# Joint P*V bursts, one pool of work banks, a split first load and a new instruction order in a fused attention and feed-forward kernel

## The chip, the cores and the metric

The kernel runs on one core of one Trainium2 chip. The metric is the device time of one execution in microseconds (us), and lower is better. The profile's span is about 2 us shorter than that time, because it runs from the first recorded instruction to the last.

The engines appear by the profile's names. PE is TensorE (PEld is its weight load), ACT is ScalarE, DVE is VectorE, POOL is GpSimd and SP is SyncE, which issues most of the transfers. PSUM is the memory, in banks, that PE writes its results to. The granted clock is the share of the full clock rate that PE was given.

## The reference, cut to what matters

The input x has 2048 tokens of 512 values. Attention has 32 heads of 16 and runs over four segments of 512 tokens, with a memory matrix carried from segment to segment. A gated feed-forward layer of width 1792 uses the same x, and a sigmoid gate per token mixes the two results.

```python
g = _sigmoid((x * gate_w).sum(-1, keepdims=True))
# a: for each segment s of 512 tokens and each of the 32 heads
logits = einsum('bhqd,bhkd->bhqk', qs, ks) * scale + mask     # causal inside the segment
p      = softmax(logits)
a_dot  = einsum('bhqk,bhkd->bhqd', p, vs)                     # "P*V" below
a_mem  = (phi(qs) @ M) / (phi(qs) @ z + 1e-6)                 # "numerator", "denominator"
o      = sigmoid(beta) * a_mem + (1 - sigmoid(beta)) * a_dot
M, z   = M + phi(ks)^T vs, z + sum(phi(ks))
a      = o @ wo
# b: the feed-forward layer
b      = (gelu(x @ w_gate) * (x @ w_up)) @ w_down
return g * a + (1 - g) * b
```

## The kernel before

**A planner orders everything.** The program is a graph of tasks. When the kernel is built, a list scheduler simulates the five engines with an estimated duration for each task, and picks the next task again and again: the one that can start first, then the one of the highest priority. What it picks becomes the fixed order of each engine's instructions, and semaphores are derived from that order. A table of small priority corrections (`BIAS`) is the outcome of a search for a short plan. A wrong duration in this model costs nothing by itself. It costs when the order it produces makes an engine stand in front of something that is not ready.

```python
while len(order) < n:
    for e in ENGINES:
        for t in ready[e]:
            st = max(cur[e], ready_at[t.id])
            if t.tiled == "pv":                       # a P*V burst: at once after a QK fill, else late
                if last_pe == "qk" and ready_at[t.id] <= cur[e]:
                    best = ((-1.0, 0.0, t.id), e, t)
                    continue
                st += t.patience
            if t.grp is not None and t.grp.bank is None:   # needs a free PSUM bank
                if not bank_free: continue
                st = max(st, min(bank_free.values()))
            k = (st, -t.prio - ..., t.id)
            ...
    if t.nbytes:
        dma_free = max(t.finish + 1.5, dma_free) + t.nbytes / DMA_RATE
```

**Attention.** A group of eight heads is handled as two units of four heads. Five "fills" of Q*K products (A0, B0, C, A1, B1) go to the four score banks. Each is followed by one exponential of 128x2048 on ACT, which writes a "P tile" to on-chip memory, and by a causal mask on POOL. C serves both units. P*V of a unit is 16 matmuls into one private PSUM bank `Pb`, followed by a DVE transpose.

```python
R_PT = 6; N_W = 3                                  # six P tiles, three work banks
Pb = psum_tensor("psP", [P, 512], F32)             # P*V's own bank
def pv(j, sa, sbk, sc):
    for kb in range(4):
        for q in range(4):
            matmul(Pb[32*q:32*q+17, 128*kb:512], Vaug[...], PT[slot][...],
                   tile_position=(0, 32*q))        # four tiles of 32 columns side by side
    task(transpose of Pb into Tb[t % 2] on DVE)
a0 = fill("A0", ...); b0 = fill("B0", ...); cc = fill("C", ...)
pv(0, a0, b0, cc)
a1 = fill("A1", ...); b1 = fill("B1", ...)
pv(1, a1, b1, cc)
norm()
```

Three tilings of the array alternate on PE: four row tiles for Q*K, four column tiles for P*V, and the whole array for everything else.

**Start.** PE runs ten warming matmuls (columns of zeros) while x arrives, transposes x, runs three more of them, and then makes the first K and Q products. Beta and the gate row are needed in odd layouts, and they are loaded by many tiny pieces on ACT's queue.

```python
wdma("wk", SP, wk[:], r4(A_wk), 524288)
wdma("wq", SP, wq[:], r4(A_wq), 524288)
wdma("wv", SP, wv[:], r4(A_wv), 524288)
wdma("beta", ACT, betab[:], A_beta.partition_broadcast(P), 8192)
for g in range(4):      # pieces of two values, 4 bytes
    bsrc = A_beta.rearrange("(t g j) -> g t j", g=4, j=2)[g]
    dma(f"betaT{g}", ACT, betaT[32*g:32*g+32, :]..., bsrc.partition_broadcast(32), 1024)
wdma("gatew", ACT, gatew[:], gate_w.rearrange("(kb p) -> p kb", p=P), 1024)   # one value, 2 bytes
```

The softmax here doesn't subtract the row's maximum and nothing guards it: scores larger than these inputs give would overflow.

## Time and profile before

| Quantity | Before | Seen in |
|---|---|---|
| median time | 293.34 us (293.33 to 293.64) | timed runs |
| traced span | 290.8 us | profile page |
| PE busy | 272.3 us, 94% | profile page |
| ACT busy, next after PE | 217.5 us, 75% | profile page |
| first exponential starts | 16.66 us | timeline |
| PE busy from 120 to 150 us | 24.88 of 30 us | windows |

These are lines of the profile page of the kernel before: busy microseconds of each engine; the busy tenths of PE and its granted clock in 40 slices of 7.3 us; and the shares, by engine, of the chain of work that ended last.

```profile
PE 272.3 (94%) x2150; PEld 114.2 (39%) x2189; DVE 191.3 (66%) x332; ACT 217.5 (75%) x172; POOL 103.0 (35%) x193
PE   6699999999999899996799999999999999999995
PEclk9899999999999999999799999999999999999999
PE 79%; DVE 9%; ACT 5%; DMA 3%; issue 2%; POOL 1%; SPq 0%; ACTq 0%
```

PE bounds the kernel: it is busy nearly always, and the chain that ended last is four fifths PE. There are two soft places, slices 1 and 2 (0 to 15 us) and slices 19 and 20 (131 to 145 us). In both the clock drops too.

The next lines are the largest waits of PE in the kernel before: what PE waited to do, for whom, the sum, the number of times and the longest.

```profile
PE psW L421 <- DVE otok L677: 3.4, 3, 2.1
PE psXALL L730 <- ACT pt L738: 2.6, 5, 1.5
PE psW L421 <- DMA wq<-in_A_wq_dram: 2.0, 1, 2.0
PE psW L516 <- DMA hT<-in_A_x_dram: 1.5, 1, 1.5
```

`otok` is the scaled numerator of the attention memory, and `hT` at the start serves as the landing place of x. The timeline of the kernel before gives start, length, engine and line, output and inputs, and in brackets the idle time before and who ended it.

```profile
7.20 0.73 PE L516 MATMUL psW<-ident,hT 128*128 128x128 bf16 x10 [1.47 <-DMA hT<-in_A_x_dram]
9.11 1.04 PE L421 MATMUL psW<-xT,wk 128*128 128x512 bf16 x4
12.19 1.89 PE L421 MATMUL psW<-xT,wq 128*128 128x512 bf16 x4 [2.04 <-DMA wq<-in_A_wq_dram]
...
137.16 0.39 PE L730 MATMUL psXALL<-qT,kpad_1 32*128 32x512 bf16 x4 [1.51 <-ACT pt L738]
...
139.61 2.34 PE L421 MATMUL psW<-xT,wu 128*128 128x512 bf16 x5 [2.05 <-DVE otok L677]
```

Four matmuls of the same form take 1.04 us at 9.11 and 1.89 us at 12.19. The difference is the clock, as the windows show. The windows give start and end in us, the length, busy time (and instructions) of PE, PEld, DVE, ACT and POOL, the granted clock, the DMA share and GB/s.

```profile
0.00:30.00 30.00, 24.72 (x156) 9.69 (x159) 15.05 (x33) 16.11 (x18) 11.52 (x33) 0.94 0.89 244
120.00:150.00 30.00, 24.88 (x232) 10.54 (x235) 25.11 (x42) 21.60 (x19) 9.81 (x13) 0.94 0.09 19
12.00:14.00 2.00, 1.81 (x5) 0.71 (x6) 0.80 (x4) 0.96 (x2) 0.00 (x0) 0.55 0.88 282
```

From the view of the transfers of the kernel before, ACT's queue q10 (packets, MB, share of the 16 engines' span) and two transfers (number, size, median us from issue to landing) matter in the argument. Only the tiny loads are on q10.

```profile
q10 hardware_dynamic: 1248, 0.01, 0.2%
...
hT<-in_A_x_dram SPq DMA_DIRECT2D x2, 256.0 KB, 5.0
...
wq<-in_A_wq_dram SPq DMA_DIRECT2D x1, 512.0 KB, 9.8
```

### The profile page before, as it was taken

The page shows a single profiled execution, that of the slowest core. Times are in us where ns is not written, and L with a number is a line of the kernel's source. Part 1 is how long each engine was busy: PE and PEld are TensorE (multiplying, and loading weights), DVE is VectorE, ACT ScalarE, POOL GpSimd, SP SyncE. Part 2 cuts the span into 40 slices and gives each one's busy share as a digit, 9 for nine tenths or more (in the row PEclk, how much of TensorE's full clock was granted, in tenths as well). Part 3 has the DMA queues.
Part 4 walks back from the last instruction along what each step waited for, and adds up shares of the span by engine and source line. Part 5 has one row for each costly group of instructions (what it writes and reads, how often), then busy time and mean ns, then how long its engine had stood idle before and what let it go on. Part 6 is the DMA issues. An engine that isn't in the chain of part 4 may idle for free.

```text
span 290.8 us, 5337 instructions
## 1 busy us (share of the span) xinstructions
PE 272.3 (94%) x2150; PEld 114.2 (39%) x2189; DVE 191.3 (66%) x332; ACT 217.5 (75%) x172; POOL 103.0 (35%) x193
## 2 busy tenths in 40 slices
PE   6699999999999899996799999999999999999995
PEld 2234343343455343432244343344344434533342
DVE  0378898885887947899451926299980767772432
ACT  2377898888998767986668878789787767777722
POOL 8015864344006353343200334366420243343320
PEclk9899999999999999999799999999999999999999
DMA  3999990000005541000200121000000000211002
GB/s 88 285 246 342 280 102 2 0 1 2 0 2 72 73 109 38 1 0 20 54 2 0 36 38 36 10 29 2 0 2 0 1 3 0 48 45 38 19 2 72
DMA packets 29737, 15.30 MB, mean 53 GB/s; under 512 B 21264, under 2 KB 29712, under 8 KB 29712
## 3 DMA queue, kind: packets, MB, share of 16 engines
q1 hardware_dynamic: 28464, 14.95, 22.5%
q8 instruction: 17, 0.28, 0.4%
q10 hardware_dynamic: 1248, 0.01, 0.2%
q14 instruction: 8, 0.07, 0.1%
HBM read 8.14 MB, written 2.10 MB: 35 GB/s over the span
## 4 chain that ended last, share of the span: by engine, by line
PE 79%; DVE 9%; ACT 5%; DMA 3%; issue 2%; POOL 1%; SPq 0%; ACTq 0%
PE psW L421 64%; PE psXALL L730 8%; PE psP L763 6%; ACT pt L738 5%; DMA wq<-in_A_wq_dram 3%; PE psXALL L421 1%; DVE tb L771 1%; DVE kpad_1 L617 1%; DVE hT L861 1%; DVE otok L677 1%; POOL pt L750 1%; DVE kT L597 1%; DVE ost L889 0%; SPq L452 0%; DVE pex L595 0%
## 5 line engine op out<-in xcount | busy, mean ns | idle before, releaser
L738 ACT ACTIVATE pt<-psXALL 128x2048 bf16<-128x2048 f32 x80 | 150.1, 1877 | 42.6 <-PE psXALL L730 27.9
L750 POOL TENSOR_SCALAR_AFFINE_SELECT pt<-pt 128x512 bf16<-128x512 bf16 (+1 forms) x112 | 83.2, 745 | 172.4 <-ACT pt L738 151.7
L421 PE MATMUL psW<-xT,wu 128*128 128x512 bf16 x216 | 52.1, 386 | 2.8 <-DVE otok L677 2.1
L861 DVE TENSOR_TENSOR hT<-psW,hT 128x512 bf16<-128x512 f32 x56 | 37.1, 686 | 26.3 <-PE psW L421 26.1
L421 PE MATMUL psW<-xT,wg 128*128 128x512 bf16 x217 | 50.7, 380 | 0.8 <-ACT hT L840 0.2
L421 PE MATMUL psW<-wd,hT 128*128 128x512 bf16 x203 | 50.5, 380 | 0.5 <-issue 0.2
L771 DVE STREAM_TRANSPOSE tb<-psP 128x512 f32<-128x512 f32 x32 | 22.9, 714 | 31.7 <-PE psP L763 31.4
L421 PEld LDWEIGHTS psW<-xT,wu 128*128 128x128 bf16 x224 | 20.5, 99 | 29.0 <-issue 3.3
L421 PEld LDWEIGHTS psW<-xT,wg 128*128 128x128 bf16 x224 | 20.5, 98 | 25.5 <-issue 1.7
L421 PEld LDWEIGHTS psW<-wd,hT 128*128 128x128 bf16 x210 | 18.8, 98 | 22.4 <-issue 3.3
L763 PE MATMUL psP<-pt,vaug 128*17 128x256 bf16 (+3 forms) x512 | 23.3, 301 | 0.6 <-POOL pt L750 0.6
L840 ACT ACTIVATE hT<-psW 128x512 bf16<-128x512 f32 x28 | 16.4, 597 | 6.7 <-PE psW L421 6.7
L421 PE MATMUL psW<-xT,wq 128*128 128x512 bf16 x59 | 16.3, 397 | 2.6 <-DMA wq<-in_A_wq_dram 2.0
L730 PE MATMUL psXALL<-qT,kpad_1 32*128 32x512 bf16 (+3 forms) x256 | 15.8, 301 | 2.6 <-ACT pt L738 2.6
L421 PE MATMUL psW<-xT,wk 128*128 128x512 bf16 x61 | 16.2, 396 | 0.3 <-DVE sc_1 L785 0.2
L421 PE MATMUL psW<-wv,xT 128*128 128x512 bf16 x61 | 15.7, 381 | 0.3 <-DVE vaug L438 0.2
L438 DVE CAST hT<-psW 128x512 bf16<-128x512 f32 x20 | 13.5, 683 | 3.8 <-PE psW L421 3.4
L730 PE MATMUL psXALL<-qT,kpad_0 32*128 32x512 bf16 (+3 forms) x256 | 15.8, 301 | 0.1
L763 PEld LDWEIGHTS psP<-pt,vaug 128*17 128x17 bf16 x512 | 10.0, 89 | 14.0 <-issue 5.9
L645 POOL COPY exsT<-exs 32x4 f32<-32x4 f32 x64 | 14.1, 220 | 3.7
L421 PE MATMUL psW<-wo,oT 128*128 128x512 bf16 x54 | 14.6, 380 | 0.6 <-issue 0.3
L829 ACT ACTIVATE hT<-hT 128x2048 bf16<-128x2048 bf16 (+2 forms) x6 | 12.7, 2185 | 0.0
(93 smaller groups left out, 242.5 us busy)
## 6 DMA issues: line engine op xcount, KB each, us to landing
out_dram<-ost SPq DMA_DIRECT2D x16, 128.0 KB, 1.7
wg<-in_B_w_gate_dram SPq DMA_DIRECT2D x2, 896.0 KB, 13.1
wu<-in_B_w_up_dram SPq DMA_DIRECT2D x2, 896.0 KB, 7.0
wd<-in_B_w_down_dram SPq DMA_DIRECT2D x1, 1792.0 KB, 13.0
hT<-in_A_x_dram SPq DMA_DIRECT2D x2, 256.0 KB, 5.0
wk<-in_A_wk_dram SPq DMA_DIRECT2D x1, 512.0 KB, 7.2
wq<-in_A_wq_dram SPq DMA_DIRECT2D x1, 512.0 KB, 9.8
wv<-in_A_wv_dram SPq DMA_DIRECT2D x1, 512.0 KB, 12.5
```

Of the source, the lines that this page charges most:

```text
L421: return Instr(lambda e: e.matmul(view(), lhsT, rhs, start=first, stop=last), reads=reads, writes=[fkey if fkey is not None else g.key], e ...
L438: alts[DVE] = [Instr(lambda e: e.tensor_copy(dst(), src()), reads=reads, writes=writes, est=dve_t(n))]
L597: Instr(lambda e: e.tensor_tensor(dst[:, t0:t1, :], dst[:, t0:t1, :], ex[:], ALU.add), dk + [("pex", i)], dk, dve_t(1024, 2))])
L645: cross = task(f"exsT{s}", POOL, [Instr(lambda e, g=g, c=c: e.tensor_copy(exsT[sl][32 * g:32 * g + 32, c:16:4], exs[32 * c:32 * c + 32, s4 ...
L730: instrs.append(Instr(lambda e, t=t, g=g, j=j, kb=kb, ncol=ncol, c0=c0: e.matmul(X[g][:, c0:c0 + ncol], kpad[j][sl][32 * g:32 * g + 32, t, ...
L738: prev_exp[0] = exp_task(s, f"exp{s}_{t}{name}", [Instr(lambda e: e.activation(PT[slot][:], XALL[:, :].rearrange("p (g c) -> p g c", g=4), ...
L750: minstrs.append(Instr(lambda e, view=view, pat=pat: e.affine_select(out=view, in_=view, compare_op=ALU.is_ge, fill=0.0, base=0, pattern=p ...
L763: instrs.append(Instr(lambda e, q=q, kb=kb, slot=slot, c0=c0, h=h: e.matmul(Pb[32 * q:32 * q + 17, 128 * kb:512], Vaug[sl][:, kb, h, :], P ...
L771: task(f"pvt{s}_{t}_{j}", DVE, [Instr(lambda e: e.transpose(Tb[i2][:, j, :], Pb[:, :]), [("P",)], [("Tb", i2, j)], dve_t(512))])
L829: t = task(f"gelu{s}_{f0}", ACT, [Instr(lambda e, hv=hv: e.activation(hv, hv, ACTF.Gelu_apprx_tanh), hk, hk, act_t(512 * n, False) + (0.0 ...
L840: lambda e, g=g, ft=ft, s=s: e.activation(hT[s % 2][:, ft, :], g.f32()[:, :], ACTF.Gelu_apprx_tanh),
L861: task(f"Um{s}_{ft}", DVE, [Instr(lambda e, g=g, ft=ft: e.tensor_tensor(hT[sl][:, ft, :], g.f32()[:, :], hT[sl][:, ft, :], ALU.mult), [g.k ...
```

## The change

The intent is to remove changes of tiling by running both units' P*V as one burst, to let every product use any of four work banks, to bring the first pieces of `wk` and `wq` early, to replace the tiny loads by contiguous ones that are spread on chip, and to give the planner truer durations and a new order.

```diff
-R_PT = 6
-N_W = 3
+R_PT = 7
+N_W = 4
-BIAS = { ... }
+BIAS = { ... }                       # wholly new: found anew
# planner: durations
-    cur = {e: 0.0 for e in ENGINES}
+    cur = {e: 0.8 for e in ENGINES}
-    dma_free = max(t.finish + 1.5, dma_free) + t.nbytes / DMA_RATE
+    dma_free = max(t.finish + 2.2, dma_free) + t.nbytes / DMA_RATE
-    Instr(lambda e: e.reciprocal(nf, nf), [("nd",)], [("nd",)], 0.3),
+    Instr(lambda e: e.reciprocal(nf, nf), [("nd",)], [("nd",)], 0.95),
# ... four more durations corrected
# planner: P*V may follow Q*K or P*V, takes a bank of the pool, and a ready pair keeps banks free
-    if last_pe == "qk" and ready_at[t.id] <= cur[e]:
+    if last_pe in ("qk", "pv") and ready_at[t.id] <= cur[e] and bank_free and \
+            min(bank_free.values()) <= cur[e]:
# P*V
-    Pb = psum_tensor("psP", [P, 512], F32)
+    gp = Grp(banks)                  # in pv(): any bank of the four
-    pv(0, a0, b0, cc)
     a1 = fill("A1", ...); b1 = fill("B1", ...)
-    pv(1, a1, b1, cc)
+    joint = [S.tasks[-1]]            # both wait for the last fill's mask
+    pv(0, a0, b0, cc, joint)
+    pv(1, a1, b1, cc, joint)
# start
-    wdma("wk", SP, wk[:], r4(A_wk), 524288)
-    wdma("wq", SP, wq[:], r4(A_wq), 524288)
+    for c0, c1 in ((0, 128), (128, 512)):
+        for key, w, src in (("wk", wk, A_wk), ("wq", wq, A_wq)):
+            wdma((key, c0 > 0), SP, w[:, :, c0:c1], r4(src)[:, :, c0:c1], ...)
-    wdma("beta", ACT, ...); 4 x dma("betaT", ACT, ...); wdma("gatew", ACT, ...)
+    wdma("gwrow", SP, gwrow[:], gate_w.rearrange("(kb p) -> kb p", p=P), 16384)   # transposed by PE
+    wdma("beta", SP, betab[:], A_beta.partition_broadcast(P), 65536)   # POOL copies make omgT
# x is transposed in the idle score banks; four of the warming matmuls go
-    x0t: g = Grp(banks) ...   -warmP, -warmE (3)
+    x0t: XB[:, kb*1024 + ...] with key ("X", kb)
```

## The prediction

> **What bounds the kernel.** TensorE. The page has PE busy 272.3 of 290.8 us and the chain of waits is 79% PE. ACT is next (217.5 us; 80 exponentials of 1.88 us = 150.1). So PE time counts: waits, slow clock, and mode switches inside "busy".
>
> Reading PE by stretches of the span (table of windows, and PE's own timeline):
> - 0 to 12.2 us: 7.2 busy. PE waits 1.47 us for x and 2.04 us (10.15 to 12.19) for `wq`, whose DMA lands 9.8 us after issue. After that hole the granted clock is 0.55 to 0.59 from 12 to 16 us: about 1.7 us more. The first exponential starts at 16.7 us.
> - 12 to 120 us: about 3.2 us of small waits.
> - 120 to 150 us: 24.9 of 30 busy, clock 0.94: holes of 1.51 and 2.05 us at 137 and 139.6 us, where the numerator products hold all three work banks and wait for DVE (`otok` copies behind a 0.95 us reciprocal that the old plan estimates at 0.3). About 5 us of wait, 1.2 us of slow clock.
> - 150 to 270 us: about 2 us. Tail after the last matmul: about 3 us.
>
> **What the change does.**
> 1. *Joint P*V.* A QK fill occupies PE 0.32 us before the next work, of which four concurrent tiles of 512 columns need 0.213; a P*V burst occupies 0.65 for 1280 columns (0.533). So each change of tiling costs about 0.11 us, in agreement with the Trainium skill, "TensorEngine Tiling (Array Packing)", Key Properties: changing the mode drains the engine. 32 bursts become 16 pairs: 16 x 0.11 = 1.8 us, all on PE, critical.
> 2. *Four shared banks.* Projections, gate, up and down products get a fourth bank while no P*V is open, but a pair takes two until its two 0.72 us transposes finish. Small net gain.
> 3. *Corrected durations and a new order.* I expect the 120 to 150 us hole to go mostly and new small ones to appear: 3 us net.
> 4. *Start.* The first 128 columns of `wk` and `wq` arrive first, so the first Q product can follow the first K product without the 2.04 us wait, and the clock should stay up: up to 3.7 us. Against it: 256-byte rows, more descriptors, three warming matmuls gone, `wv` later. Net 3 us. The tiny pieces for beta and gate leave the queues; exponentials start about 4 us earlier.
> 5. *Losses.* The last pair's two transposes run one after the other before the last normalisation: +0.7 us in the tail, partly covered by the last down products. New GpSimd copies and the single `Tb` are off the path (DVE 66% busy).
>
> Sum: 1.8 + 0.5 + 3 + 3 - 0.7 = 7.6 us off 293.3.
>
> **Prediction: 285.7 us, range 281.5 to 290. Faster by over 2%: 0.70; within 2%: 0.27; slower: 0.03.**
>
> **What would show it.** (1) P*V groups in pairs of about 1.2 us, 16 of them; (4) first `wq` matmul near 10 us, clock not below 0.9 from 10 to 16 us, first exponential near 12.5 us; (3) PE busy over 28.5 of 30 us in every 30 us window of the middle; (5) last matmul to end of span as before, or under 1 us more. PE idle over the span should fall from 18.5 to about 12 us.
>
> **What would make it wrong.** The clock drops anyway in the start because the warmers are gone or the rest of `wk`/`wq` (768-byte rows) lands late; the pair, which waits for both units' exponentials and masks and for two banks, makes PE or ACT stall elsewhere; the new order merely moves the mid holes.

## The result, and the profile after

The kernel after takes **278.41 us** (278.16 to 278.99, four runs), against 293.33 us in the same rounds (293.25 to 293.64). The ratio is 0.9492, with a 95% interval of 0.9476 to 0.9509. That is 14.9 us saved, where 7.6 us had been predicted; the measured time lies 3 us below the range.

These lines of the page of the kernel after answer to those of the page before.

```profile
PE 265.9 (96%) x2147; PEld 114.8 (41%) x2186; DVE 196.7 (71%) x336; ACT 213.1 (77%) x166; POOL 101.5 (37%) x197
PE   8999999999999999999999999999899999999995
PEclk9999999999999999999999999999999999999999
PE 81%; ACT 6%; DVE 4%; POOL 2%; issue 2%; DMA 2%; SPq 1%; DVEq 0%; ACTq 0%; POOLq 0%
```

Both soft places are gone and the clock is full wherever it was recorded. (The trace's clock records begin at 5.5 us, and at 5.4 us before; earlier the view shows 1.00 without one, while in both kernels the warming matmuls start 0.43 us apart, against 0.22 later on.) PE still bounds the kernel. PE idle fell from 18.5 to 10.8 us, and PE busy fell by 6.4 us: slow-clock matmuls and changes of tiling sit inside "busy". The two together are the 14.1 us of span.

These are the largest waits of PE in the kernel after; "issue" means that the profile shows nothing that PE waited for.

```profile
PE psW L430 <- issue: 2.7, 17, 0.2
PE psW L513 <- DVE pt L488: 1.3, 1, 1.3
PE psW L430 <- DVE hT L873: 1.1, 3, 0.6
PE psXALL L741 <- ACT pt L749: 0.5, 2, 0.3
PE psW L430 <- DMA wq<-in_A_wq_dram: 0.3, 1, 0.3
```

After the start almost nothing is left to wait for. The first line is mostly not real: these 17 gaps of 0.16 us are places where the record of one matmul is missing (of the program's 937 matmuls of 512 columns over the whole array, the trace has 898). The timeline of the kernel after shows the start, and then one joint pair with such a gap behind it.

```profile
5.07 1.27 PE L518 MATMUL psXALL<-ident,hT 128*128 128x128 bf16 x16
...
6.36 0.61 PE L430 MATMUL psW<-xT,wk 128*128 128x512 bf16 x2
...
6.80 0.59 PE L430 MATMUL psW<-xT,wq 128*128 128x512 bf16 x2
...
52.40 1.26 PE L774 MATMUL psW<-pt,vaug 128*17 128x512 bf16 x32
...
53.59 0.55 PEld L430 LDWEIGHTS psW<-xT,wg 128*128 128x128 bf16 x4 [0.16 <-issue]
53.83 0.81 PE L430 MATMUL psW<-xT,wg 128*128 128x512 bf16 x3 [0.16 <-issue]
```

x is transposed 2.1 us earlier than before, and the first Q product comes at 6.80 instead of 12.19 us. The pair of P*V occupies PE from 52.40 to about 53.6 us, 1.20 us. Behind it four weight loads stand against three matmuls: the fourth matmul ran and was not recorded.

The windows of the kernel after, for the same two long stretches as before:

```profile
0.00:30.00 30.00, 28.06 (x220) 12.20 (x225) 19.57 (x42) 21.59 (x22) 19.32 (x63) 1.00 0.98 288
120.00:150.00 30.00, 28.60 (x262) 13.53 (x263) 21.33 (x42) 22.77 (x24) 10.73 (x32) 1.00 0.09 19
```

The start has gained 3.3 us of PE busy time in 30 us and the stretch from 120 to 150 us 3.7. These are the same two transfers in the kernel after; that of `wq` is its first part.

```profile
hT<-in_A_x_dram SPq DMA_DIRECT2D x2, 256.0 KB, 3.0
...
wq<-in_A_wq_dram SPq DMA_DIRECT2D x1, 128.0 KB, 4.4
```

**An account of PE's loss.** From the length of each stretch I took off the time that its matmuls need merely to stream their columns (0.216 us for an ordinary matmul of 512 columns, a quarter of that where four tiles run side by side). Matmuls without a record were counted from the program's order. What is left is loss: waits, slow clock and changes of tiling.

| Stretch | lost before | lost after |
|---|---|---|
| 0 to 20 us | 9.8 us | 4.8 us |
| 20 to 120 us | 10.8 us | 8.2 us |
| 120 to 150 us | 9.45 us | 3.1 us |
| 150 us to the end | 14.5 us | 15.1 us |

Four warming matmuls fewer add 0.9 us, since before they counted as work. So 5 to 6 us came from the start, 6 from the stretch from 120 to 150 us, and about 2 from the rest.

### The profile page after: what moved, and what is told of

Its sections match the earlier page's. It is cut to its first block, busy times and chain, and to the rows that moved or that the text cites. A ratio compares the mean times of both kernels' runs of the same rounds, so it can differ in the third digit from the quotient of the medians.

```text
span 276.7 us, 5333 instructions
## 1 busy us (share of the span) xinstructions
PE 265.9 (96%) x2147; PEld 114.8 (41%) x2186; DVE 196.7 (71%) x336; ACT 213.1 (77%) x166; POOL 101.5 (37%) x197
## 4 chain that ended last, share of the span: by engine, by line
PE 81%; ACT 6%; DVE 4%; POOL 2%; issue 2%; DMA 2%; SPq 1%; DVEq 0%; ACTq 0%; POOLq 0%
PE psW L430 65%; PE psXALL L741 8%; PE psW L774 6%; ACT pt L749 5%; DMA wq<-in_A_wq_dram 2%; PE psXALL L430 1%; POOL exsT L656 1%; SPq L461 1%; POOL pt L761 1%; DVE hT L873 1%; ACT L852 1%; DVE ost L901 1%; DVE tb L782 0%; ACT hT L852 0%; DVE ndsc L678 0%
## 5 line engine op out<-in xcount | busy, mean ns | idle before, releaser
L761 POOL TENSOR_SCALAR_AFFINE_SELECT pt<-pt 128x512 bf16<-128x512 bf16 (+1 forms) x112 | 81.1, 727 | 156.0 <-ACT pt L749 134.0
L430 PE MATMUL psW<-xT,wu 128*128 128x512 bf16 x216 | 51.3, 380 | 1.4 <-DVE hT L873 0.6
L873 DVE TENSOR_TENSOR hT<-psW,hT 128x512 bf16<-128x512 f32 x56 | 37.3, 685 | 15.2 <-PE psW L430 13.6
L782 DVE STREAM_TRANSPOSE tb<-psW 128x512 f32<-128x512 f32 x32 | 21.1, 697 | 21.6 <-PE psW L774 21.4
L774 PE MATMUL psW<-pt,vaug 128*17 128x256 bf16 (+3 forms) x512 | 20.4, 300 | 0.2 <-ACT hT L852 0.2
L430 PE MATMUL psW<-xT,wq 128*128 128x512 bf16 x59 | 15.7, 380 | 0.8 <-DMA wq<-in_A_wq_dram 0.3
L430 PE MATMUL psW<-wo,oT 128*128 128x512 bf16 x57 | 15.1, 380 | 0.2
L656 POOL COPY exsT<-exs 32x4 f32<-32x4 f32 x64 | 13.8, 216 | 3.7
L774 PEld LDWEIGHTS psW<-pt,vaug 128*17 128x17 bf16 x512 | 10.7, 90 | 10.5 <-issue 3.5
L901 DVE TENSOR_SCALAR ost<-psW,omgt 128x512 bf16<-128x512 f32 x10 | 7.3, 748 | 9.8 <-PE psW L430 9.8
```

What stands on the lines that cost most here:

```text
L430: return Instr(lambda e: e.matmul(view(), lhsT, rhs, start=first, stop=last), reads=reads, writes=[fkey if fkey is not None else g.key], e ...
L656: cross = task(f"exsT{s}", POOL, [Instr(lambda e, g=g, c=c: e.tensor_copy(exsT[sl][32 * g:32 * g + 32, c:16:4], exs[32 * c:32 * c + 32, s4 ...
L761: minstrs.append(Instr(lambda e, view=view, pat=pat: e.affine_select(out=view, in_=view, compare_op=ALU.is_ge, fill=0.0, base=0, pattern=p ...
L774: instrs.append(Instr(lambda e, q=q, kb=kb, slot=slot, c0=c0, h=h: e.matmul(gp.f32()[32 * q:32 * q + 17, 128 * kb:512], Vaug[sl][:, kb, h, :],
L782: task(f"pvt{s}_{t}_{j}", DVE, [Instr(lambda e: e.transpose(Tb[:, j, :], gp.f32()[:, :]), [gp.key], [("Tb", j)], dve_t(512))], grp=gp)
L873: task(f"Um{s}_{ft}", DVE, [Instr(lambda e, g=g, ft=ft: e.tensor_tensor(hT[sl][:, ft, :], g.f32()[:, :], hT[sl][:, ft, :], ALU.mult), [g.k ...
```

## The experiments

All experiments except four keep an order. For these, the planner's choice was replaced by a list of (task, engine, bank), recorded from the kernel before or after. The list reproduces that kernel exactly, so that only the edit differs. There is one exception: in `b_tiny`, `b_start` and `b_both` the work on beta of ACT and DVE also moves behind the first copies of K and Q. In the kernel before ACT waits 2.86 us for the beta pieces, until 11.58 us, before it copies the first K product; PE's wait for `wq`, until 12.19 us, ends later.

```diff
-    for t in S.schedule():
+    for t in S.replay(ORDER):       # ORDER: the recorded choice of the kernel before, or after
```

In the other four ("order found anew") the search for `BIAS` was run again. "Saved" is (1 - ratio) times 293.34 us. Each ratio is against the kernel before in the same rounds. Four executions stand behind each row, three behind the row of `a_pair1`.

| Run | Base, order | Edit | Median us | Ratio [95%] | Saved us |
|---|---|---|---|---|---|
| after | | the whole change | 278.41 | 0.9492 [0.9476, 0.9509] | 14.9 |
| b_tiny | before, kept | small loads as in the change | 289.86 | 0.9887 [0.9869, 0.9905] | 3.3 |
| b_split | before, kept | `wk`, `wq` split | 295.38 | 1.0072 [1.0031, 1.0113] | -2.1 |
| b_start | before, kept | both | 290.49 | 0.9911 [0.9889, 0.9933] | 2.6 |
| b_pool | before, kept | P*V in one pool of four banks | 289.82 | 0.9883 [0.9865, 0.9901] | 3.4 |
| b_both | before, kept | start and pool | 285.79 | 0.9753 [0.9713, 0.9793] | 7.2 |
| b_retuned | before, anew | true durations | 291.21 | 0.9917 [0.9879, 0.9955] | 2.4 |
| b_start_retuned | before, anew | true durations and start | 281.00 | 0.9571 [0.9532, 0.9610] | 12.6 |
| b_retuned_oldstart | that order, kept | old start put back | 286.77 | 0.9774 [0.9735, 0.9813] | 6.6 |
| a_pair1 | after, kept | pairs apart by 1 piece | 281.64 | 0.9597 [0.9581, 0.9613] | 11.8 |
| a_pair2 | after, kept | pairs apart by 2 pieces | 282.13 | 0.9616 [0.9600, 0.9632] | 11.3 |
| a_unsplit | after, kept | `wk`, `wq` whole | 283.61 | 0.9665 [0.9627, 0.9703] | 9.8 |
| a_addtiny | after, kept | old small loads added on ACT | 283.56 | 0.9678 [0.9647, 0.9710] | 9.4 |
| a_tinylate | after, kept | the same on SP, behind `wv` | 283.35 | 0.9650 [0.9601, 0.9698] | 10.3 |
| a_addbetaT | after, kept | only the beta pieces added | 281.36 | 0.9581 [0.9543, 0.9619] | 12.3 |
| a_oldstart | after, kept | old start put back | 288.85 | 0.9836 [0.9791, 0.9881] | 4.8 |
| a_nojoin | after, anew | P*V not joint | 279.71 | 0.9531 [0.9500, 0.9563] | 13.8 |
| a_oldtimes | after, anew | old durations | 280.94 | 0.9579 [0.9548, 0.9611] | 12.3 |

The theories were these. J: a joint pair is worth its saved changes of tiling, some 0.1 us each as predicted. S: the start is worth more than predicted, and it is the tiny pieces (rival: the split of `wk` and `wq`) that make it so. O: the plan with true durations holds on the chip, where the old plan did not (rival: the pool of banks alone cures the hole at 120 to 150 us).

### The start, one half at a time, in the order of before

```diff
# b_tiny
-    wdma("beta", ACT, ...); 4 x dma("betaT", ACT, ...); wdma("gatew", ACT, ...)
+    wdma("gwrow", SP, ...); wdma("beta", SP, ...)      # behind wv; spread on chip as in the change
# b_split
-    wdma("wk", SP, wk[:], ...); wdma("wq", SP, wq[:], ...)
+    wk[:, :, 0:128], wq[:, :, 0:128], wk[:, :, 128:512], wq[:, :, 128:512]     # four loads
# b_start: both
```

> The kernel before with its order of work kept as a fixed list, and only the beta and gate loads changed as in the change (one row load each behind wv on the SP queue, spread on chip); no split of wk and wq. Theory T (the tiny loads on the second queue held up the x and weight loads): x is transposed from about 5 us instead of 5.5 to 8.6, the first wk matmul starts near 7 instead of 9.1 us, total 1.5 to 2.5 us less (near 291). Rival S (only the order of wk and wq matters): x and wk land as before, total within 0.5 us of 293.3.

> The kernel before, order kept, and only wk and wq loaded in two parts (first 128 columns of both first). Rival S: first wq matmul follows the first wk one with no wait, clock stays up, total about 3.5 us less (near 290). Theory T: x still ends near 8.5 us, so about 2 us less, the rest needs the tiny loads gone.

> The kernel before, order kept, with both start changes. The account of PE time lost in the first 20 us is 9.8 before and 4.8 after, plus 0.9 for four warming matmuls that stay here. If the start is worth what this account says and all of it reaches the end, total 4 to 5.5 us less (288 to 289). If work later absorbs it (a fixed order tuned for a late start), under 2.5 us less.

Without the tiny pieces x lands 2.9 us after issue instead of 5.0, and 3.3 us are saved. The transfers of `b_tiny`:

```profile
hT<-in_A_x_dram SPq DMA_DIRECT2D x2, 256.0 KB, 2.9
```

The split alone makes the kernel 2.1 us slower. With the tiny pieces still there, `wv` lands 9.4 us after its issue, PE then waits 2.0 us for it at 15.2 us, and the clock falls to 0.50 from 16 to 20 us. Both halves together save 2.6 us in this order, no more than the small loads alone. The mean granted clocks of the timed runs show where some of it goes. The time lost to the clock, (1 - clock) times the span, is about 3.5 us before, 1.7 in `b_tiny`, 5.3 to 7.1 in `b_split` and 3.5 to 3.8 in `b_start`. That is enough to account for all that the split lost, and for `b_start` not beating `b_tiny`. The soft stretch from 120 to 150 us is not healed: in `b_start` PE is as busy there as before, and the clock is 0.89 instead of 0.94.

```profile
120.00:150.00 30.00, 24.95 (x209) 9.89 (x211) 21.90 (x38) 20.14 (x19) 8.14 (x11) 0.89 0.09 19
```

### The pool of banks, in the order of before

```diff
-N_W = 3                          Pb: private
+N_W = 4                          gp = Grp(banks) in pv(), as in the change
# b_both: this and b_start's edit
```

> The kernel before, order kept, P*V takes its bank from one pool of four (no joint bursts, six P tiles). Theory P (the hole of 120 to 150 us in the kernel before is a shortage of banks): the waits for otok at 97 and 139 us shrink, total about 2 to 3 us less. Rival O (the hole comes from the order and the DVE chain, banks matter little once the order is fixed): within 1 us of before.

> The kernel before, its order kept, with both start changes and the pool of four banks; no joint bursts, six P tiles. If the two parts add (b_start gave about -2.6 us, b_pool -3.2): about 287.5. If the pool lets the earlier start reach the end: 285 to 286.5. What stays between this run and 278.4 is the joint burst (1.8 to 3.2 by the split-pair runs) and the order.

The pool alone saves 3.4 us. The wait for `otok` at 97 us is gone, and that at 137 us is 0.68 instead of 2.05 us. But 120 to 150 us is not healed: PE is busy for 26.18 of 30 us and the clock is 0.94. The wait for ACT's exponential stays, with 1.78 us instead of 1.51:

```profile
135.18 0.39 PE L882 MATMUL psXALL<-qT,kpad 32*128 32x512 bf16 x4 [1.78 <-ACT pt L890]
```

Start and pool together save 7.2 us in the old order, about half of the whole. So about half needed something else of the change, such as the joint form or a new order.

### Is the joint burst worth its changes of tiling?

```diff
# a_pair1, a_pair2: in the recorded order of the kernel after
-  ... qk1_1B0  pv0_0_0  pv0_0_1  G1_6.0  G1_5.2 ...
+  ... qk1_1B0  pv0_0_0  G1_6.0  pv0_0_1  G1_5.2 ...     # one piece (2 matmuls) between; a_pair2: two
```

> The changed kernel, its order kept, but the second P*V of each of the 16 pairs moved one piece of ordinary products (two matmuls, 0.43 us) later on PE. Theory J (a pair saves one change of tiling of about 0.11 us, and a split pair pays two more): total 1.8 to 3.4 us more than the changed kernel (280.2 to 281.8). Rival Q (the pair gains nothing: in the changed kernel a pair takes 1.42 us up to the next ordinary product at the median, two single bursts of the kernel before 2 x 0.65, because PE then sits 0.16 us with nothing issued): total within 1 us of 278.4.

> The same with two pieces (0.86 us) between the two bursts. Theory J: as with one piece, 280.2 to 281.8. Rival Q: within 1 us of 278.4. More than 1 us over the run with one piece would mean that the later transpose delays something on DVE, and not the tiling.

Taking the pairs apart costs 3.1 and 3.6 us. This is the timeline of `a_pair2` around the pair shown above:

```profile
52.68 0.72 PE L934 MATMUL psW<-pt,vaug 128*17 128x512 bf16 x16
...
53.34 1.04 PE L590 MATMUL psW<-xT,wg 128*128 128x512 bf16 x4
...
54.30 0.72 PE L934 MATMUL psW<-pt,vaug 128*17 128x512 bf16 x16
...
54.96 0.29 PE L901 MATMUL psXALL<-qT,kpad 32*128 32x256 bf16 x4
```

Behind the second burst the next Q*K fill follows here at once, so that only one change of tiling is added in this place. Counted over the whole program (consecutive matmuls on PE whose tilings differ), before has 195 changes, after 181, `a_pair1` 211 and `a_pair2` 200. Fifteen pairs are joined; the last two bursts, at 265.36 and 267.42 us, are apart in the kernel after too.

Thirty more changes cost `a_pair1` 3.1 us, which is 0.10 us for each, if they are all of it. That agrees with the 0.11 us of the prediction. `a_pair2` has only 19 more and is still 3.6 us slower, so there is a second cost. Its span is 280.3 us against 276.7, and its PE busy time grew by 2.4 us (268.3 against 265.9), which is 0.13 us a change; PE idle grew by 1.2 us. Among its waits are 0.5 us for `oT`, 0.4 for `mzbd` and 0.3 for `tb`, all behind DVE, which are not among those of after. That the later burst makes DVE late is likely, but it was not tested. `a_pair1` left no profile to look for the same in.

The Trainium skill, "TensorEngine Tiling (Array Packing)", Key Properties, says that a change of tiling mode drains the array. Runs agree, with 0.10 to 0.13 us a change.

Two remarks belong here. The expectation of `a_pair1` read the 0.16 us gap behind the pair as time in which nothing was issued. It is a missing record, as shown above, and the pair takes 1.20 us and not 1.42. And the profiled execution of `a_pair1` took 679.3 us: its ordinary matmuls of 512 columns took about 820 ns in the mean instead of 380, while DVE and ACT were busy as long as ever. It did not come again, and its profile is not used; three timed executions (281.4 to 281.7 us) remain.

### What is the joint burst worth when the order may adapt?

```diff
# a_nojoin, order found anew
-            joint = [S.tasks[-1]]
+            joint = []
```

> The changed kernel without the joint burst (each P*V of its own, after its own unit's fills), with pool, start and corrected durations, order found anew by search for this form. Theory J (one change of tiling of 0.11 us per pair, 1.8 us, plus what the order loses): 280 to 282. Rival: within 1 us of 278.4.

279.71 us, 13.8 us saved, is only 1.1 us worse than the whole change. The search finds an order with 193 changes of tiling, 12 more than after, and at 0.10 us each these are 1.2 us. So the joint form is worth 1.1 us with the freedom that the change itself had, and taking pairs apart in a fixed order overstates it.

### The start, in the order of after

```diff
# a_unsplit: the queue is then wk, gate row, beta, wq, wv
-    for c0, c1 in ((0, 128), (128, 512)): ...
+    wdma("wk", SP, wk[:], ...); wdma("wq", SP, wq[:], ...)
# a_addtiny: the six small loads of before, first on ACT's queue, into tiles that nothing else uses
+    wdma("betaX", ACT, ...); 4 x dma("betaT", ACT, ...); wdma("gateX", ACT, ...)
# a_tinylate: the same six on SP, behind wv            a_addbetaT: only the four betaT, on ACT
# a_oldstart: a_unsplit and a_addtiny together
```

> The changed kernel, its order kept, wk and wq loaded whole again (wk, gate row, beta, wq, wv). If the split matters as the prediction said, PE waits for wq by about 2 us near 7 us and the clock may drop: 2 to 4 us more (280.5 to 282.5). If the tiny loads were the whole of the late start: under 1.2 us more.

> The changed kernel, its order kept, with the beta and gate loads of the kernel before added again at the head of the ACT queue, into tiles that only three small GpSimd copies at the end read. Theory T: x lands about 2 us later (first x transposes done after 7.5 us instead of 6.3), wk and wq later too, total 2 to 4 us more. Rival: under 0.7 us more.

> The changed kernel, its order kept, with the same old small loads added, but on the SP queue behind wv. If their place ahead of x, wk and wq is what costs: within 1 us of 278.4, x lands 3 us after issue as in the changed kernel. If the pieces cost wherever they stand: 2 us or more, since wg and the next x land later.

> The changed kernel, its order kept, with only the four loads of beta in four-byte pieces (1024 pieces) added at the head of the ACT queue. If these are the main cost of the small loads: 3 to 5 us more than 278.4 and x lands 4.5 us or more after issue. If the broadcast and the gate row matter as much: under 2 us more.

> The changed kernel, its order kept, with both start changes undone: wk and wq whole, and the old small loads at the head of the ACT queue. If the two parts overlap (either alone makes PE wait and its clock drop once): 5 to 6.5 us more than 278.4 (283.5 to 285). If they add: about 10 us more (288).

In the order of after each half is needed. Without the split the first Q product waits until 11.13 us and the clock is at 0.50 to 0.55 from 10 to 16 us: 5.1 us lost.

```profile
11.13 1.03 PE L590 MATMUL psW<-xT,wq 128*128 128x512 bf16 x2 [2.47 <-DMA wq<-in_A_wq_dram]
```

Not all of this need be the split. With the order kept, the gate row and beta now stand between `wk` and `wq`: `wq` landed at 11.08 us here and at 9.36 in `b_tiny`, where nothing stands between them. How the 5.1 us divide was not tested. With the old tiny loads added, x lands 4.6 us after issue and the first parts of `wk` and `wq` after 5.8 and 7.6 us: 5.5 us lost. Counted in the profile, the six small loads are 1,248 packets and the four of beta alone 576 (where an expectation gives another number of pieces, the profile's count holds). The transfers of `a_addtiny` and then of `a_addbetaT`:

```profile
hT<-in_A_x_dram SPq DMA_DIRECT2D x2, 256.0 KB, 4.6
```

```profile
hT<-in_A_x_dram SPq DMA_DIRECT2D x2, 256.0 KB, 4.5
```

These pieces run on ACT's queue, and x on SP's. That they delay it all the same agrees with the Trainium skill, "DMA: Bandwidth & Descriptors", Issuing engines are not separate DMA queues: transfers end on the same 16 DMA engines whoever starts them. The same page, Rules for kernel authors, says that a strided last dimension becomes one descriptor per element, and tells one to make it contiguous. The change does that, and the packets of these loads agree: 672 of the 1,248 are left for the 512 single values of the gate row and one row of beta for each of 128 partitions. What the page doesn't give is what such a load costs those behind it. `a_tinylate` shows it. I expected it to lose under 1 us if only the place of the small loads mattered. It lost 4.6 us. These are its windows from 10 to 14 us (the last two figures are DMA share and GB/s), and then one of its waits of PE.

```profile
10.00:12.00 2.00, 2.00 (x28) 1.01 (x29) 1.84 (x5) 1.32 (x2) 0.88 (x4) 1.00 0.12 19
12.00:14.00 2.00, 2.00 (x17) 0.87 (x10) 0.42 (x2) 1.62 (x1) 1.51 (x9) 1.00 0.05 0
```

```profile
PE psW L595 <- DMA wg<-in_B_w_gate_dram: 1.9, 1, 1.9
```

For 4 us the queues moved almost nothing, with the engines' share of time at 0.05 to 0.12, and `wg`, which stood behind the pieces, came late: PE waited for it until 22.59 us. So the pieces cost wherever they stand ahead of something that is needed. The beta pieces alone cost 2.6 us, about half.

`a_oldstart` undoes both halves and loses 10.1 us. PE waits 4.1 us for `wq` and 1.6 for `wk`, and from 10 to 12 us nearly nothing runs:

```profile
10.00:12.00 2.00, 0.52 (x2) 0.00 (x0) 0.00 (x0) 0.00 (x0) 0.00 (x0) 0.50 0.52 153
```

This probably overstates the start: the order of after takes K and Q products by turns and has no warming matmuls to bridge the wait, and, as in `a_unsplit`, the gate row and beta stand ahead of `wq`, which landed at 14.53 us instead of 12.14 before. Which measure is fair is settled by the next group.

### Order and start apart

```diff
# b_retuned: before, only the planner's durations corrected as in the change, BIAS found anew
# b_start_retuned: before's banks, six P tiles, single P*V and warming matmuls;
#                  durations corrected, both start changes, BIAS found anew
# b_retuned_oldstart: b_start_retuned's order kept, the start loads of before put back
# a_oldtimes: after, the planner's durations as before, BIAS found anew
```

> The kernel before with nothing of the start, the pool or the joint bursts: only the durations of the planner corrected as in the change, and the order found anew by the same kind of search over the bias table. Theory O (an order planned with true durations is worth much by itself): 284.5 to 288, the hole of 120 to 150 us mostly gone. Rival B (the gain is in the banks, the start and the joint bursts; order is only the remainder): 290 to 293.5.

> The kernel before (private bank for P*V, three work banks, six P tiles, warming matmuls) with both start changes, corrected durations, and an order found anew by the same search. Against a_nojoin (279.7: pool of four, seven P tiles). If the pool is worth in a fitted order what it was in the old one (3.2 us): 282.5 to 284. If a fitted order makes three banks enough: within 1 us of 279.7.

> The order of b_start_retuned kept, but wk and wq whole and the old small loads at the head of the ACT queue again. If order and start add, and b_retuned was a poor order: 5 to 7 us more than 281.0 (286 to 288), nearly all of it lost in the first 20 us, the stretch 120 to 150 us still full. If the order is only good with its own start: 290 or more, with holes again after 20 us.

> The changed kernel with the old planner durations (reciprocal 0.3 instead of 0.95 us and so on), order found anew by search against them (its own planner says 274.1, the changed kernel's says 274.2). Theory O2 (true durations make the plan hold on the chip): 281 us or more. Rival: the durations are details, within 1 us of 278.4.

`b_retuned` saved only 2.4 us, and for a while that spoke against theory O. Its plan was 279.0 us and its span 289.6: it had put Q first, so that PE waits 1.9 us for `wk`, and the stretch from 120 to 150 us still lost 2.7 us. `b_start_retuned` then saved 12.6 us without a joint burst, pool or seventh tile; its span, 279.1 us, is its plan's 279.2. `b_retuned_oldstart` decides between "the new order needs the new start" and "they add". It keeps that order with the old start and still saves 6.6 us. Its windows, after those of `b_start_retuned`:

```profile
0.00:30.00 30.00, 28.75 (x200) 11.88 (x201) 18.01 (x35) 22.65 (x23) 13.56 (x31) 1.00 1.04 294
120.00:150.00 30.00, 30.00 (x219) 13.20 (x217) 20.93 (x37) 23.78 (x24) 6.37 (x9) 1.00 0.01 1
```

```profile
0.00:30.00 30.00, 24.35 (x145) 9.57 (x146) 12.89 (x27) 17.25 (x19) 11.03 (x28) 0.94 0.90 252
120.00:150.00 30.00, 29.98 (x224) 12.39 (x224) 22.60 (x39) 23.85 (x24) 8.69 (x11) 1.00 0.01 1
```

These two profiles hold all 941 matmuls of 512 columns. That alone makes PE look up to 0.5 us busier in 30 us than in the profile of after, where 39 are missing. That of `b_start_retuned` has no clock record either; its matmuls of 512 columns start 0.216 us apart from 4.7 us on, so the clock was full.

The middle stays full whatever the start does, and the start is as soft as it was before. So the order is worth 6.6 us with the old start, and the start 6.0 us more on top of it (2.6 us in the old order). The latter agrees with the account of PE's loss (5.0 us in the first 20 us, plus 0.9 for the warming matmuls). `b_retuned` was one poor order of one search, which is why one order should not stand for "true durations". The same holds for the good one: with true durations and the old start loads, these two orders differ by 4.2 us.

`a_oldtimes` has everything of the change except the durations. It is 2.6 us slower than after, though its plan looks no worse. It is the only run that takes away the durations alone, again with one new search:

| Kernel | planned | span measured |
|---|---|---|
| before | 279.25 us | 290.8 us |
| b_retuned | 279.0 us | 289.6 us |
| b_start_retuned | 279.2 us | 279.1 us |
| a_oldtimes | 274.1 us | 279.7 us |
| a_nojoin | 276.6 us | 278.1 us |
| after | 274.2 us | 276.7 us |

The plan of before falls behind by 6.1 us within the first 15.6 us, with x late by 1.65 us, `wq` by 2.20 and the slow clock behind that, and again at 34, 97 and 139 us. After never slips by more than 1.2 us before its end. Of the 14.1 us of span, 9.1 are a plan that now holds, and 5.0 a shorter plan. This is bookkeeping and not a cause: the two plans are made with different durations, and that of before starts 0.8 us earlier.

A longer search from after's order found no shorter plan, so no further kernel was run to beat it.

## Why the prediction was right or wrong

The direction was right and the size was wrong: 285.7 us predicted, 278.41 measured, below the range of 281.5 to 290. By one chain of experiments (order, then start, then layout, then joint), the 14.9 us divide as follows.

| Term | Predicted us | Measured us | From |
|---|---|---|---|
| order found anew with true durations | 3 | 6.6 | b_retuned_oldstart |
| start | 3 | 6.0 | b_start_retuned less that |
| banks, with seventh P tile, score-bank transposes, no extra warmers | 0.5 | 1.2 | a_nojoin less b_start_retuned |
| joint P*V | 1.8 | 1.1 | after less a_nojoin |
| tail | -0.7 | about 0 | trace |

The shares depend on the order in which they are taken. In the old order the pool alone is worth 3.4 us, and in the fixed new order the joint form 3.1. By the intervals of the two runs behind it, the third row (1.2 us) may be zero, and the fourth (1.1 us) is only just not. Each row with an order found anew also holds the luck of one search, and the searches of `b_retuned` and `b_start_retuned`, planned for different start loads, led to orders that on the old start are 4.2 us apart. Against that the third and fourth rows are small.

1. **Joint P*V.** Right in mechanism and size: a pair takes 1.20 us as expected and a change of tiling 0.10 us or a little more. There are 15 pairs and not 16, and 14 changes fewer than before (181 against 195), where I had counted 16. Once the order may adapt, 1.1 us remain of the 1.8.
2. **Four shared banks.** "Small net gain" holds once the order is planned anew. That the pool would be worth 3.4 us in the old order, by ending the waits for `otok`, was not seen.
3. **Corrected durations and a new order.** This is one of the two steps that failed: "3 us net" was mis-sized. I read a hole of about 6 us at 120 to 150 us and assumed that "new small ones" would take half of it back. Hardly any came: the changed kernel's plan holds on the chip, and apart from the start PE waits about 2 us in all. I also put both waits in the hole down to the work banks and `otok`; the one of 1.51 us ended on ACT's exponential, and the pool did not end it. That true durations are why the new order holds is shown only in part: without them a new search lost 2.6 us (`a_oldtimes`), and `b_retuned` had them and still fell 10.6 us behind its plan. The test that I named, PE busy for more than 28.5 of 30 us in every middle window, came true (28.60 to 29.75), and the new order measured 6.6 us.
4. **Start.** This is the other mis-sized step: "net 3 us" measured 6.0. The place was right and the cause only half. I credited the split of `wk` and `wq` and treated the tiny pieces as a side matter. The pieces delay x itself, which lands after 3.0 instead of 5.0 us, and they delay every weight load behind. The split alone loses 2.1 us (`b_split`). I expected the first `wq` matmul near 10 us and the first exponential near 12.5; they came at 6.80 and 9.64 us. The feared losses (clock without warmers, 768-byte rows) did not come: the clock is 1.00 wherever it was recorded.
5. **Tail.** Wrong in kind. The last pair is not joined, so its transposes don't run one after the other. From the last matmul's start to the end of the span it is 3.6 us against 3.4 before.

On the clock: the Trainium skill, "TensorE: Matmul & The Clock Gate", Part 1, says that an idle window of about 3.4 us halves the clock and about as much sustained work brings it back. The traces agree about half speed and its length: 0.55 and 0.59 granted from 12 to 16 us before work out as 3.4 us at half clock. But a wait of 2.04 us, with 1.47 us idle a little earlier, was enough here. The windows after it are part of what the start was worth, and the prediction did count them, as 1.7 us.

**What stays open.** The worth of the seventh P tile, of the score-bank transposes and of the dropped warming matmuls was not measured one by one (the joint form needs seven tiles: five of its own and two of the next group that already stand before the pair). Why the search behind `b_retuned` ended in a poor order is not known. How much of the order's 6.6 us is due to the true durations, and how much to a longer or luckier search, is not known either: no kernel was run with the banks and start of before, the old durations and a new search. How the cost of the small loads divides beyond the half that is beta's was not measured.

## What to carry to other kernels

When a kernel's order is planned from estimated durations, compare the plan with the traced span first: the gap (11.6 us here) shows where wrong durations and late loads upset it, and an order that closes the gap can be worth more than the structural change beside it (6.6 us against 1.1). Do not judge by one search, since two led to orders 4.2 us apart. Look for small strided loads ahead of the first large ones, on any queue, because a few kilobytes in pieces of 2 and 4 bytes delayed 256 KB loads by 2 us here. And judge one part of a change with the order both kept and planned anew, since a fixed order overstated (3.1 against 1.1 us) or understated (2.6 against 6.0 us) what a part was worth.

## What the Trainium skill lacked or had wrong

- "DMA: Bandwidth & Descriptors" says that a strided last dimension costs one descriptor per element, but not what that costs others. Here 1,248 packets (0.01 MB) delayed x on another queue from 3.0 to 4.6 us and the kernel by 5.5 us; placed later on the same queue as the weights they cost 4.6 us, with 19 and 0 GB/s moved in two windows of 2 us.
- "TensorE: Matmul & The Clock Gate", Part 1, gives an idle window of about 3.4 us for the clock to halve, and says that short idle times between groups of matmuls can do it too, but not how much idle time is enough. Here a wait of 2.04 us, after an idle 1.47 us some 3 us before, was followed by 3.4 us at half clock.
- "TensorEngine Tiling (Array Packing)" says that a change of mode drains the array, without a figure. Here it costs 0.10 to 0.13 us.
- I know of no page that tells how to recognise a missing matmul record in the timeline: here a gap of 0.16 us put down to "issue", with one weight load more than matmuls, 17 times in the kernel after.
- No page describes what one execution of `a_pair1` showed: 679.3 us against 281.6, with ordinary matmuls of about 820 ns in the mean instead of 380 and other engines unchanged. The nearest is the remark in "TensorE: Matmul & The Clock Gate", Part 1, that the clock gate has been seen stuck at a quarter for over 50 us. Here matmuls of 512 columns mostly started 0.62 us apart, against 0.216 at full clock, all through the execution. That is a third of the rate and not a quarter, and the profile has no clock record.
